# A fused attention and two-layer kernel: the first stage rebuilt, with two blocks in float32 and row scale and squares taken where the results leave PSUM

## The chip, the cores and the metric

One Trainium2 chip, of which the program uses one core. The metric is device time in microseconds (us) of one execution; less is better. The comparison can tell about 0.2% (2 us here) from no change.

## The reference, cut to what matters

```python
for t in range(S):                       # B=4, H=8, S=768, D=48
    state = alpha[:, :, t, :, None] * state + einsum('bhd,bhe->bhde', k[:, :, t], v[:, :, t])
    y[:, :, t] = einsum('bhd,bhde->bhe', q[:, :, t], state)
x = y as 3072 tokens x 384
xn = x / sqrt(mean(x * x, axis=-1) + 1e-6) * rms_g
g = xn @ w_gate                          # 384 x 1536
x = (g / (1 + exp(-g)) * (xn @ w_val)) @ w_out
h = x @ w_in                             # 384 x 2048
out = (h * cos(h)) @ w_out2
```

The weights reach the kernel as 64-bit floats, everything else as 32-bit floats.

## The kernel before, in words

The 3072 tokens are eight tiles of 384. **Attention** of a tile is four units, each a pair of heads on 112 partitions (48, a gap of 16, 48). For unit u, `att_prep` (letter p) multiplies up the decays with two scans on VectorE and scales k and q; `att_T` (T) transposes k, `att_sc0` (s) makes the scores in two PSUM banks, which ScalarE copies out and GpSimd masks; `att_u` (u) makes the state of each 128-token block, with a carry to the next tile; `att_y` (y) makes the result in PSUM and copies it into the tile `xT`, rows 0 to 47 on ScalarE, rows 64 to 111 on VectorE. The first unit of a tile (heads 6 and 7) is spread by six small DMAs (`att_fix`) over the gaps of the other three, so that `xT` has three blocks of 128 rows.

**The first layer** of a tile runs over twelve blocks f of 128 hidden columns: a gate product `pg`, a value product `pv`, Silu and product on ScalarE and VectorE, and a product into three sums `o`. Every operand is split into a high and a low word (type F32R, `xh`, `xl`, `hh`, `hl`, `g0h`, `g0l` and so on), and one product is three matmuls; a gate or value product is nine matmuls of 384 columns, an output product of one block nine too. For tiles 0 to 2 the row factor (`rms`) is multiplied in after the gate product, so that the products needn't wait for it.

**Weights** come in pieces of 768 or 384 64-bit numbers per partition (`st_g`, `st_v`, `st_o`, later `ws`). `conv_a` makes 32-bit numbers of one: ScalarE scales the low words, then the high words, VectorE joins both (`cv`). `conv_b` splits that: ScalarE copies the high word (`g0h`), VectorE subtracts for the low word (`g0l`). The second half of the first three pieces is hidden blocks 2 and 3; the pieces g1, v1, o1 follow, and those of blocks 8 to 11 (g2, v2, o2) come through three `ws` buffers, each loaded when VectorE has joined what was in it.

**Order.** The string `FIRST` is the order of tile 0's pieces, held on every engine; `i` in it is filler matmuls (`keep_clock`). After it, a counter of slots deals out conversions (`CONV`) and the attention of the next tile between the blocks of the current one. What stands in which order on an engine within these limits is decided when the program is built. SyncE issues all loads of this stage, in order.

The second layer follows from about 500 us on and isn't touched.

## Time and profile before

| | us |
|---|---|
| median of 3 runs (lowest to highest) | 995.41 (995.2 to 995.5) |
| the profiled execution, its own time | 995.65 |
| its span, first to last instruction | 993.9 |
| outside the span | 1.75 |

The rows below are of this one execution. Busy times of TensorE include a modelled tail of each matmul, so a busy TensorE may still have room; the distance between the starts of two matmuls is what one costs in a row of them.

### The profile page before, as it was taken

How to read it: one execution, taken by the hardware profiler on the slowest of the kernel's cores; microseconds unless marked ns; L12 is line 12 of the kernel's file. 1: busy time of each engine (PE TensorE's matmuls, PEld its weight loads, DVE VectorE, ACT ScalarE, POOL GpSimd, SP SyncE). 2: the span in 40 equal slices, each digit the busy share in tenths (PEclk: the TensorE clock that was granted, in tenths of full speed). 3: DMA queues.
4: the chain of work that ended last, by engine and by line, in shares of the span. 5: the costliest groups of instructions: out<-in, count | busy, mean ns of one | idle time of the engine just before them, and what ended most of it. 6: DMA issues, size and time to landing. Idle time of an engine off the chain costs nothing.

```text
span 993.9 us, 16981 instructions
## 1 busy us (share of the span) xinstructions
PE 976.8 (98%) x6451; PEld 900.6 (91%) x6451; DVE 707.3 (71%) x1333; ACT 608.8 (61%) x1270; POOL 119.1 (12%) x154
## 2 busy tenths in 40 slices
PE   8799999999999999999999999999999999999998
PEld 7698899999999999999999998888888888888886
DVE  7898786978868678678537227777767777777666
ACT  4878465565664565555633227777777677777764
POOL 3010010100110010010102211121201201211000
PEclk9999999999999999999999999999999999999999
DMA  8937234443453443544202574001010010000000
GB/s 244 328 93 203 83 92 138 125 132 93 124 152 121 135 131 102 146 137 126 89 18 88 200 305 170 18 28 38 1 43 22 1 54 12 32 1 1 33 1 32
DMA packets 44273, 96.71 MB, mean 97 GB/s; under 512 B 5520, under 2 KB 25488, under 8 KB 44192
## 3 DMA queue, kind: packets, MB, share of 16 engines
q1 hardware_dynamic: 41312, 79.90, 26.3%
q0 software_dynamic: 2880, 15.73, 4.3%
q8 instruction: 51, 0.84, 0.4%
q14 instruction: 30, 0.25, 0.1%
HBM read 69.26 MB, written 25.17 MB: 95 GB/s over the span
## 4 chain that ended last, share of the span: by engine, by line
PE 87%; DVE 6%; DMA 3%; ACT 2%; issue 1%; SPq 0%; POOL 0%; DVEq 0%; ACTq 0%; POOLq 0%
PE p L838 20%; PE pg L700 13%; PE o L700 12%; PE pv L700 12%; PE px L838 9%; PE py L838 9%; PE py L481 2%; PE pe L838 2%; DMA q<-akq 2%; PE py L486 1%; PE pu L448 1%; PE idle L534 1%; DVE cv L189 1%; PE ps L382 1%; PE ps L383 1%
## 5 line engine op out<-in xcount | busy, mean ns | idle before, releaser
L838 DVE SCALAR_TENSOR_TENSOR kk<-kk,c 128x512 f32<-128x512 int32 x192 | 148.4, 773 | 93.2 <-ACT kk L838 93.2
L838 PE MATMUL p<-hh,p 128*128 128x512 f32 x576 | 211.5, 396 | 0.2 <-ACT kk L838 0.2
L838 PEld LDWEIGHTS p<-hh,p 128*128 128x128 f32 x576 | 108.7, 189 | 17.1 <-ACT kk L838 0.3
L838 ACT ACTIVATE kk<-kk 128x512 f32<-128x512 f32 x192 | 115.7, 626 | 3.0
L838 PE MATMUL p<-hl,p 128*128 128x512 f32 x288 | 113.7, 395 | 0.2 <-DVE hl L89 0.2
L838 PE MATMUL px<-xh,i 128*128 128x256 f32 x481 | 113.8, 291 | 0.0
L838 PE MATMUL py<-xh,i 128*128 128x256 f32 x482 | 109.4, 282 | 0.0
L399 POOL TENSOR_SCALAR_AFFINE_SELECT sm<-sm 128x512 f32<-128x512 f32 (+1 forms) x64 | 47.6, 747 | 454.1 <-ACT sm L398 454.0
L838 PEld LDWEIGHTS px<-xh,i 128*128 128x128 f32 x481 | 84.2, 189 | 12.3 <-ACT py L838 12.3
L759 DVE TENSOR_TENSOR pv<-th,pv 128x384 f32<-128x384 f32 x96 | 53.3, 555 | 58.6 <-PE pv L700 51.0
L86 ACT ACTIVATE hh<-pv 128x384 fp32r<-128x384 f32 x96 | 46.9, 488 | 67.5 <-DVE pv L759 65.3
L838 PEld LDWEIGHTS py<-xh,i 128*128 128x128 f32 x482 | 84.3, 189 | 4.3 <-DVE hl L89 0.3
L746 ACT ACTIVATE th<-pg 128x384 f32<-128x384 f32 x96 | 46.8, 488 | 65.3 <-PE pg L700 45.8
L89 DVE TENSOR_TENSOR hl<-kk,hh 128x512 fp32r<-128x512 f32 x96 | 68.1, 710 | 3.3
L838 PE MATMUL px<-xl,i 128*128 128x256 f32 x240 | 67.8, 283 | 0.0
L838 PE MATMUL py<-xl,i 128*128 128x256 f32 x240 | 67.6, 282 | 0.0
L89 DVE TENSOR_TENSOR hl<-pv,hh 128x384 fp32r<-128x384 f32 x96 | 53.0, 552 | 18.3 <-ACT hh L86 17.2
L838 ACT ACTIVATE kk<-c 128x512 int32<-128x512 f32 x96 | 60.3, 628 | 1.6
L838 PEld LDWEIGHTS p<-hl,p 128*128 128x128 f32 x288 | 54.4, 189 | 5.6 <-DVE hl L89 1.0
L838 ACT ACTIVATE m<-pe 128x256 f32<-128x256 f32 x48 | 18.4, 384 | 53.8 <-PE pe L838 53.8
L838 PEld LDWEIGHTS py<-xl,i 128*128 128x128 f32 x240 | 45.2, 189 | 4.3
L838 ACT ACTIVATE c<-px 128x512 f32<-128x512 f32 x48 | 28.8, 599 | 31.7 <-PE px L838 31.6
(233 smaller groups left out, 2623.3 us busy)
## 6 DMA issues: line engine op xcount, KB each, us to landing
ak<-akq SPq DMA_DIRECT2D x29, 337.8 KB, 3.5
i<-d_i POOLq DMA_DIRECT2D x12, 768.0 KB, 6.0
ws<-w2i SPq DMA_DIRECT2D x16, 384.0 KB, 3.4
ws<-w2o SPq DMA_DIRECT2D x16, 384.0 KB, 3.4
d_p<-whl SPq DMA_DIRECT2D x32, 192.0 KB, 3.2
p<-d_p POOLq DMA_DIRECT2D x8, 768.0 KB, 6.4
v<-vin SPq DMA_DIRECT2D x32, 168.0 KB, 3.4
q<-akq SPq DMA_DIRECT2D x30, 168.0 KB, 3.0
```

Of the source, the lines that this page charges most:

```text
L86: return act.activation(out=dst, in_=src, func=AF.Copy)
L89: return eng.tensor_tensor(out=dst, in0=a, in1=h.bitcast(F32), op=ALU.subtract)
L189: done("dve", dve.scalar_tensor_tensor(out=v, in0=hi, scalar=3, in1=lo, op0=ALU.logical_shift_left, op1=ALU.bitwise_or))
L382: pe.matmul(dst, a[0], b[0], start=start, stop=False)
L383: pe.matmul(dst, a[0], b[1], start=False, stop=False)
L399: pool.affine_select(out=dst, in_=dst, pattern=[[0, n], [1, C]], compare_op=ALU.is_ge, fill=0.0, base=0, channel_multiplier=-1,)
L448: done("pe", pe.matmul(pu[r0:r1, n * D:(n + 1) * D], s["t"][:, n * R + r0:n * R + r1], s["v"][:, n, r0:r0 + D], start=True, stop=True,))
L481: pe.matmul(py[r0:r1, c], s["v"][:, n, r0:r1], s["s"][:, n, j, :], start=n == 0, stop=False)
L700: mm(dst, w[a][:, cols(kc)], rhs[kc][b], start=first and k == 0, stop=last and k == 3 * len(rhs) - 1,)
L746: done("act", act.activation(out=t, in_=p, func=AF.Silu, scale=1.0 / WS))
L759: dve.tensor_tensor(out=p, in0=t, in1=p, op=ALU.mult)
L838: last2[eng] = fn(*args, **kw).ins
```

## The change

What it does:

- Blocks 0 and 1 of tile 0 are computed in float32: the joined weights (`whole`, held in three buffers that are free at this time) and `xT` go straight into three float32 matmuls for each gate and value product, and one for each of the three output sums. Their result `hh` is written by VectorE as float32, without a split. The split of these three half pieces for the later tiles is done by `conv_whole` at slots 9, 11 and 13, and slot 0 has no conversion now.
- The row scale `rms_g` is multiplied in where tile 0's `att_y` copies PSUM out, so `x_split` of tile 0 is a plain copy and a subtraction. The first unit's scale has a layout of its own, `g3`, which six small DMAs on ScalarE's queue load; all of its rows are copied out by ScalarE.
- The squares of tile 0 are taken by ScalarE from PSUM for each of the four units, so the row sum has four parts of 112 rows and doesn't wait for `att_fix`.
- The carry of tile 0 (the last state update of each unit) is left to the end of the first stage (`carry_on`, C).
- The high words of a piece can be converted ahead of its low words (`high_first`, H). `FIRST` is a new string: among other things `i5` is `i3` and `i7` is gone, and blocks 0 and 1 are finished in it (M).
- For tiles 1 and 2 the row sum is placed ahead of the first value product instead of behind it; tile 2's first state product is placed one slot later.

The diff, cut:

```diff
-    "p0 T0 s0 i4 p1 u0 i5 p2 T1 s1 y0 S4 u1 p3 T2 s2 a0 y1 u2 T3 s3 u3 b0 a1 y2 y3 i7 x0 x1 x2 b1 g0 "
-    "q0 q1 q2 r0 r1 r2 n0 a2 a3 v0 g1 o0 P0 b2 v1 P1 b3"
+    "p0 T0 s0 i4 p1 u0 i3 T1 s1 p2 y0 S4 u1 T2 s2 p3 y1 u2 T3 s3 u3 a0 y2 H0 y3 a1 g0 r0 r1 "
+    "r2 r3 a2 n0 v0 x0 x1 x2 H0 b2 g1 o0 P0 a3 v1 M0 H0 b3 P1 M1 a4 C0"
-CONV = {0, 1, 4, 6, 8, 10, 12, 14} | set(range(16, 36))
+CONV = {1, 4, 6, 8, 10, 12, 14} | set(range(16, 36))
...
+    def conv_high(st):
+        g = st.bitcast(F32).rearrange("p (n t) -> p n t", t=2)[:, :, 1]
+        done("act", act.activation(out=g, in_=g, func=AF.Prelu, scale=HIGH_SCALE, alpha=NEG_SCALE))
+
+    def high_first():
+        st = staged[0][2]
+        conv_high(st)
+        highs.append(st)
...
+        first = key[1] == "0" and o == 0
+        v = at.tile([128, 768], I32, tag=dict(g="bdh", v="bdl", o="yn")[key[0]], name="whole") if first else cv_tile(st)
...
+    def conv_whole():
+        h, l, v = whole.pop(0)
+        split(h, l, v.bitcast(F32))
...
+            if n == 2 and i == 0:
+                carried.append((p, st[-1], s["ge"], w))
+                continue
...
-            done("act", act.activation(out=x[0:D, p, :], in_=py[0:D, :TT], func=AF.Copy))
-            done("dve", dve.tensor_copy(out=x[64:R, p, :], in_=py[64:R, :TT]))
+            if u == 0:
+                done("act", act.activation(out=x[:R, p, :], in_=py[:R, :TT], func=AF.Copy, scale=g3[:R]))
+            else:
+                done("act", act.activation(
+                    out=x[0:D, p, :], in_=py[0:D, :TT], func=AF.Copy, scale=g_sb[0:D, p:p + 1]
+                ))
+                done("dve", dve.tensor_scalar(
+                    out=x[64:R, p, :], in0=py[64:R, :TT], scalar1=g_sb[64:R, p:p + 1], scalar2=None, op0=ALU.mult
+                ))
+            t = m1.tile([128, TT], F32, tag="t" if u else "y", bufs=3 if u else 1, name="sq")
+            done("act", act.activation(out=t[:R], in_=py[:R, :TT], func=AF.Square))
...
+        if full(i, f):
+            w = wt0[a]
+            for kc in range(3):
+                o = c * 384 + kc * 128
+                done("pe", pe.matmul(p[:, :TT], w[:, o:o + 128], xT[0][:, kc, :], start=kc == 0, stop=kc == 2))
+            return p
...
+            pe.matmul(acc1[i][j][:, :TT], wt0["o"][:, k], h, start=start, stop=stop)
...
-    for u in range(4):
-        load_all(u)
+    for c in range(3):
+        for r in (0, 64):
+            act.dma_start(out=g3[r + 16 * c:r + 16 * c + 16], in_=g_in[r + 48:r + 64, c:c + 1])
+    att_load(0)
+    att_loadq(0)
+    att_load(1)
+    att_loadv(0)
+    att_loadq(1)
+    att_loadv(1)
     sp.dma_start(out=g_sb, in_=g_in)
+    load_all(2)
+    load_all(3)
...
+        if i == 0:
+            done("act", copy_r(xh[:, c, :], x))
+            done("dve", sub_r(dve, xl[:, c, :], x, xh[:, c, :]))
+            return
...
-                for x in range(2):
+                for x in order1(i)[:2]:
                     pre["g", x] = m1_mm(i, "g", x, ps_g.tile([128, 512], F32, tag="g", name="pg"))
-                    if x == 0:
-                        pre["v", 0] = m1_mm(i, "v", 0, ps_g.tile([128, 512], F32, tag="g", name="pv"))
                     late.pop(0)()
+                    if x == f:
+                        pre["v", f] = m1_mm(i, "v", f, ps_g.tile([128, 512], F32, tag="g", name="pv"))
...
+        if step[0] in (9, 11, 13):
+            with behind():
+                conv_whole()
```

Three places in the order of the instructions. The first is SyncE's queue at the program's start: `ak` and `akq` hold decays, k (and q) of a unit, in the order of units 0 to 3. Before:

```order
L332 DMA v<-vin 128x336
L314 DMA ak<-akq 112x772
L323 DMA q<-akq 112x384
L332 DMA v<-vin 128x336
L312 DMA akq<-akq 112x1156
L332 DMA v<-vin 128x336 [waits DMAHW0_49]
L312 DMA akq<-akq 112x1156 [waits DMAHW1_49]
L332 DMA v<-vin 128x336 [waits DMAHW2_49]
```

And now:

```order
L338 DMA ak<-akq 112x772
L356 DMA v<-vin 128x336 [waits DMAHW0_49]
L347 DMA q<-akq 112x384 [waits DMAHW2_49]
L356 DMA v<-vin 128x336 [waits DMAHW4_49]
L1093 DMA g_sb<-gin 128x3 [waits DMAHW5_49]
L336 DMA akq<-akq 112x1156 [waits DMAHW6_49]
L356 DMA v<-vin 128x336 [waits DMAHW7_49]
L336 DMA akq<-akq 112x1156 [waits DMAHW0_49]
```

Unit 1's `ak` stands one place earlier, unit 2's `akq` waits for a semaphore that counts unit 1's `ak` (the waits named DMAHW are for the earlier DMA that shares one of eight semaphores), and the loads behind it wait in order.

The second place is ScalarE between the last scores of tile 0 (`sm`) and the row sum's copy `nm`. Before:

```order
L398 ACTIVATE sm<-ps 128x3x128 [waits PE_49,Pool_49]
L398 ACTIVATE sm<-ps 128x3x128 [waits PE_49]
L86 ACTIVATE g0h<-cv 128x768 [waits DVE_49]
L186 ACTIVATE st_v_162<-st_v_162,low 128x768 [waits DMAHW5_49]
L188 ACTIVATE st_v_162<-st_v_162 128x768
L502 ACTIVATE xT<-py 48x384 [waits PE_49] x2
L602 ACTIVATE xh<-xT,g_sb 128x384 [waits DMAHW6_49,DMAHW7_49,DMAHW3_49,DVE_49]
L602 ACTIVATE xh<-xT,g_sb 128x384 [waits DMAHW1_49,DMAHW0_49,DVE_49]
L602 ACTIVATE xh<-xT,g_sb 128x384 [waits DMAHW3_49,DMAHW2_49,DVE_49]
L86 ACTIVATE v0h<-cv 128x768
L518 ACTIVATE sq<-xT 128x384 x3
L551 ACTIVATE nm<-rm,eps 128x96 [waits PE_49]
```

And now:

```order
L428 ACTIVATE sm<-ps 128x3x128 [waits PE_49]
L199 ACTIVATE st_g_166<-st_g_166,low 128x768 [waits DMAHW2_49]
L189 ACTIVATE st_g_166<-st_g_166 128x768
L546 ACTIVATE xT<-py,g_sb 48x384 [waits PE_49]
L553 ACTIVATE sq<-py 112x384 [waits DVE_49]
L189 ACTIVATE st_v_170<-st_v_170 128x768 [waits DMAHW3_49]
L546 ACTIVATE xT<-py,g_sb 48x384 [waits PE_49]
L553 ACTIVATE sq<-py 112x384 [waits DVE_49]
L199 ACTIVATE st_v_170<-st_v_170,low 128x768
L199 ACTIVATE st_g_274<-st_g_274,low 128x768 [waits DMAHW2_49]
L189 ACTIVATE st_g_274<-st_g_274 128x768
L603 ACTIVATE nm<-rm,eps 128x96 [waits PE_49]
```

Each unit's copy `xT` is now followed by a square that waits for VectorE's copy of the other rows, five conversions of 768 columns stand among them and ahead of `nm`, and `xh` and the split copies have moved behind it.

The third place is TensorE at the state product `pu` of tile 1's last unit, while tile 0's blocks 8 to 10 are computed. Before:

```order
L700 MATMUL pv_1220<-xl_415,v2h_813 128x384
L700 MATMUL pv_1220<-xh_414,v2l_814 128x384
L700 MATMUL o0_718<-hh_1165,o2h_902 128x384
L700 MATMUL o1_719<-hh_1165,o2h_902 128x384
L700 MATMUL o2_720<-hh_1165,o2h_902 128x384
L448 MATMUL pu_949<-v_802,th_909 64x48
L448 MATMUL pu_949<-v_802,th_909 48x48
```

And now, from behind the three matmuls `o<-hh,o2h` of the same block:

```order
L760 MATMUL pg_1205<-xh_456,g2h_681 128x384
L760 MATMUL pg_1205<-xl_457,g2h_681 128x384
L760 MATMUL o0_685<-hl_1127,o2h_863 128x384
L760 MATMUL o0_685<-hh_1126,o2l_864 128x384
L760 MATMUL o1_686<-hl_1127,o2h_863 128x384
L760 MATMUL o1_686<-hh_1126,o2l_864 128x384
L760 MATMUL o2_687<-hl_1127,o2h_863 128x384
L760 MATMUL o2_687<-hh_1126,o2l_864 128x384
L760 MATMUL pg_1205<-xh_456,g2l_682 128x384
L760 MATMUL pg_1205<-xh_456,g2h_681 128x384
L760 MATMUL pg_1205<-xl_457,g2h_681 128x384
L486 MATMUL pu_910<-v_765,th_870 64x48
```

Eleven matmuls of the first layer now stand between those three and `pu`, where none stood.

## Rows read from the trace of the kernel before

**Rows 1.** The page, parts 1 and 2: engines, and granted clock in slices.
```profile
PE 976.8 (98%) x6451; PEld 900.6 (91%) x6451; DVE 707.3 (71%) x1333; ACT 608.8 (61%) x1270; POOL 119.1 (12%) x154
PEclk9999999999999999999999999999999999999999
```

**Rows 2.** Windows: busy us of each engine, granted clock, DMA share.
```profile
19.60:30.00 10.40, 9.29 (x116) 7.16 (x117) 8.52 (x17) 9.31 (x19) 1.38 (x3) 1.00 0.93 342
40.00:50.00 10.00, 8.01 (x42) 7.12 (x43) 10.00 (x18) 10.00 (x17) 0.00 (x0) 1.00 0.90 330
50.00:60.00 10.00, 10.00 (x66) 9.20 (x65) 9.60 (x17) 6.64 (x12) 1.13 (x2) 1.00 0.28 99
80.00:90.00 10.00, 9.10 (x59) 8.60 (x59) 7.47 (x15) 8.06 (x21) 2.27 (x2) 1.00 0.77 219
90.00:100.00 10.00, 9.14 (x63) 7.74 (x64) 8.31 (x20) 7.92 (x18) 0.52 (x1) 0.83 0.77 205
```

**Rows 3.** TensorE's waits, 20 to 50 us: first and last of seven.
```profile
PE pg L700 <- ACT g0h L86: 1.1, 1, 1.1
PE pg L700 <- DVE g0l L89: 0.4, 1, 0.4
```

**Rows 4.** Timeline 0 to 20 us: start, duration, engine, line, operation.
```profile
4.08 0.43 SPq L312 DMA_DIRECT2D akq<-akq  x1
7.76 0.96 DVE L347 TENSOR_TENSOR_SCAN G<-ak,d 112x387 f32<-112x387 f32 x1 [1.30 <-DMA ak<-akq]
11.72 0.96 DVE L347 TENSOR_TENSOR_SCAN G<-akq,d 112x387 f32<-112x387 f32 x1
14.97 0.56 DVE L503 COPY xT<-py 48x384 f32<-48x384 f32 x1
16.21 0.27 DVE L458 SCALAR_TENSOR_TENSOR c<-w,ge 112x48 f32<-112x48 f32 x1
18.91 0.69 DVE L356 TENSOR_TENSOR akq<-akq 112x384 f32<-112x384 f32 x1
```

**Rows 5.** DMA issued at 4.08 us: KB, us to landing.
```profile
akq<-akq SPq DMA_DIRECT2D x1, 505.8 KB, 7.2
```

**Rows 6.** Timeline and one tile: prices of matmuls and conversions.
```profile
88.41 0.33 PE L700 MATMUL pv<-xh,v2h 128*128 128x384 f32 x1
88.59 0.33 PE L700 MATMUL pv<-xl,v2h 128*128 128x384 f32 x1
L584 PE MATMUL rm<-sq,mean x12: 483/484/591, 183.4 to 521.1; 128*128 128x384 f32 x12
41.86 1.01 ACT L186 ACTIVATE st_g<-st_g,low 128x768 int32<-128x768 uint32 x1
42.76 0.92 ACT L188 ACTIVATE st_g<-st_g 128x768 f32<-128x768 f32 x1
41.89 1.80 DVE L189 SCALAR_TENSOR_TENSOR cv<-st_o 128x768 int32<-128x768 int32 x2
```

**Rows 7.** Timeline, ScalarE: tile 0's row sum and first Silu.
```profile
29.84 0.34 ACT L551 ACTIVATE nm<-rm,eps 128x96 f32<-128x96 f32 x1 [0.49 <-PE rm L543]
35.53 0.49 ACT L746 ACTIVATE th<-pg 128x384 f32<-128x384 f32 x1 [0.87 <-DVE pg L744]
```

**Rows 8.** Timeline and a window, TensorE, 88 to 95 us.
```profile
88.76 0.34 PE L700 MATMUL pv<-xh,v2l 128*128 128x384 f32 x1
90.04 0.79 PE L700 MATMUL o<-hh,o2h 128*128 128x384 f32 x3 [0.94 <-ACT hh L86]
91.66 0.66 PE L448 MATMUL pu<-v,th 128*64 128x48 f32 x8 [0.82 <-ACT th L394]
95.00 0.44 PE L700 MATMUL pg<-xh,g2h 128*128 128x384 f32 x1
92.00:93.00 1.00, 1.00 (x16) 1.00 (x15) 1.00 (x4) 1.00 (x3) 0.00 (x0) 0.50 0.76 61
```

**Rows 9.** Timeline, TensorE: tile 1's row factors.
```profile
117.63 0.89 PE L573 MATMUL rb<-yb,ones 128*128 128x384 f32 x2 [0.59 <-DVE yb L564]
```

More of the change, by code (lines that the diff above doesn't have):

```diff
@@ L75, in fused_kernel @@
     sd = []
+    yn = []
     def make_bd():
         for i in range(1):
-            bd.append([at.tile([R, NB, 2, C], F32R, name=f"bd{x}{i}") for x in "hl"])
+            bd.append([at.tile([R, NB, 2, C], F32R, tag=f"bd{x}", name=f"bd{x}{i}") for x in "hl"])
             for t in bd[-1]:
@@ L99, in fused_kernel @@
     mean = const.tile([128, 128], F32, name="mean")
+    g3 = const.tile([128, 1], F32, name="g3")
     d1 = const.tile([R, NB, C + 1], F32, name="d1")
@@ L186, in assemble @@
         act.activation(out=lo, in_=lo.bitcast(U32), func=AF.Identity, scale=LOW_SCALE, bias=low)
-        g = hi.bitcast(F32)
-        done("act", act.activation(out=g, in_=g, func=AF.Prelu, scale=HIGH_SCALE, alpha=NEG_SCALE))
+        if st in highs:
+            highs.remove(st)
+        else:
+            conv_high(st)
         done("dve", dve.scalar_tensor_tensor(
@@ L200, in fused_kernel @@
     half = []
+    whole = []
+    wt0 = {}
     def conv_a():
@@ L206, in conv_a @@
         h, l = (x[:, o:o + st.shape[-1]] for x in wt[key][0])
-        v = cv_tile(st)
+        first = key[1] == "0" and o == 0
+        v = at.tile([128, 768], I32, tag=dict(g="bdh", v="bdl", o="yn")[key[0]], name="whole") if first else cv_tile(st)
+        if first:
+            wt0[key[0]] = v.bitcast(F32)
         assemble(st, v)
-        half.append((h, l, v))
+        (whole if first else half).append((h, l, v))
         if tag and tag != "ws":
@@ L355, in att_prep @@
         q3 = q.rearrange("p (n c) -> p n c", c=C)
[L356 to L357 removed]
+        if u >= 4:
+            dve.tensor_tensor(out=k3, in0=k3, in1=Iv.rearrange("p (n c) -> p n c", c=C + 1)[:, :, 1:], op=ALU.mult)
+        ge = at.tile([R, NB, 1], F32, tag="ge" if u >= 4 else "ge0", bufs=3 if u >= 4 else 4, name="ge")
         done("act", copy_r(ge, G[:, :, C:C + 1]))
[L359 removed]
+        ins = dve.tensor_tensor(out=q3, in0=q3, in1=G[:, :, 1:], op=ALU.mult)
+        if u < 4:
+            ins = dve.tensor_tensor(
+                out=k3, in0=k3, in1=Iv.rearrange("p (n c) -> p n c", c=C + 1)[:, :, 1:], op=ALU.mult
+            )
+        done("dve", ins)
         s.update(ge=ge, k=k, q=q)
@@ L438, in att_sc0, with carry_on @@
             causal(sm[:, :, j, :], ps[:, :TT].rearrange("p (n c) -> p n c", c=C), NB)
+    carried = []
+    def carry_on():
+        for p, x, ge, w in carried:
+            done("dve", dve.scalar_tensor_tensor(
+                out=carry[p], in0=x, scalar=ge[:, 2, :], in1=w[:, 2], op0=ALU.mult, op1=ALU.add
+            ))
     def att_u(u):
@@ L716, in fused_kernel, with order1, full, parts_w @@
     acc1 = {}
+    def order1(i):
+        return list(range(12))
     pre = {}
     post = []
+    def full(i, f):
+        return i == 0 and f < 2
+    def parts_w(key, f):
+        return wt[key][0]
     def m1_mm(i, a, f, p):
         g, c = divmod(f, 4)
+        if full(i, f):
[4 more added lines that the diff above has]
+            return p
         rhs = [(xn[i][0][:, kc, :], xn[i][1][:, kc, :]) for kc in range(3)]
         mm9(
-            p[:, :TT], wt[f"{a}{g}"][0], rhs, True, True,
+            p[:, :TT], parts_w(f"{a}{g}", f), rhs, True, True,
             lambda kc: slice(c * 384 + kc * 128, c * 384 + kc * 128 + 128),
@@ L757, in m1_val @@
         hh = m1.tile([128, TT], F32R, tag="hh", bufs=3, name="hh")
+        if full(i, f):
+            done("dve", dve.tensor_tensor(out=hh.bitcast(F32), in0=t, in1=p, op=ALU.mult))
+            hid1[i, f] = hh.bitcast(F32)
+            return
         hl = m1.tile([128, TT], F32R, tag="hl", bufs=3, name="hl")
@@ L764, in m1_unit @@
         g, c = divmod(f, 4)
-        if j == 0 and f == 0:
+        start, stop = f == order1(i)[0], f == order1(i)[-1]
+        if j == 0 and start:
             acc1[i] = [ps_o.tile([128, 512], F32, tag=f"o{n}", name=f"o{n}") for n in range(3)]
-        w = wt[f"o{g}"][0]
+        w = parts_w(f"o{g}", f)
         h = hid1[i, f]
         k = slice(c * DM + j * 128, c * DM + j * 128 + 128)
-        mm9(acc1[i][j][:, :TT], w, [h], f == 0, f == 11, lambda kc: k, mm or pe.matmul)
-        if f == 11:
+        if full(i, f):
+            pe.matmul(acc1[i][j][:, :TT], wt0["o"][:, k], h, start=start, stop=stop)
+        else:
+            mm9(acc1[i][j][:, :TT], w, [h], start, stop, lambda kc: k, mm or pe.matmul)
+        if stop:
             o = m1.tile([128, TT], F32, tag="t", bufs=3, name="x2")
@@ L785, in m1_out @@
             m1_unit(i, f, j)
-        if f == 11 and i < NRAW:
+        if f == order1(i)[-1] and i < NRAW:
             rms.pop(i)
```

48 lines of the change are left out of this document (28 added, 20 removed).

## The prediction

> **What bounds the kernel now.** I read the page first: TensorE is busy for 98% of the span [rows 1], so time can only go where it waits or does work that can be spared. The windows then show where it waits: until some 120 us. From 19.6 to 30 us it lacks 1.1 us of the window, from 40 to 50 us 2.0 us; from 50 to 60 us nothing is left, and from 80 to 100 us it lacks 1.8 us again [rows 2]. The view of TensorE's waits names the releasers between 20 and 50 us: seven, all products of the weight conversion, the splits or Silu on ScalarE and VectorE, 5.1 us in all [rows 3]. Both these engines are busy for the whole of 40 to 50 us [rows 2]: the first stage is bound by the conversion of weights, not by matmuls. Last I read TensorE's timeline around the hole at 90 us. The block's last value matmul starts at 88.76 us, the next gate product at 95.00 us, and between them stand three output matmuls, `pu` and the results `py` of one unit [rows 8]. It waits 0.94 us for `hh` and 0.82 us for `th`, both of which stand in ScalarE's queue among conversions. The window from 92 to 93 us has a granted clock of 0.50, the lower of TensorE's two levels (1.2 GHz), after 2.6 us in which it had done one us of work. The 2.98 us from the start of `py` (0.36 us after that of `pu`, at 92.02) to 95.00 would have taken half, so the clock cost some 1.5 us. The waits, the clock and what little stands between them make about 3.5 us lost of the 5.9 us from 89.1 to 95.0 us: the three matmuls cost 0.5 us and `pu` with `py` at the full clock 1.9 us (0.36 and 1.5 us).
>
> **The start.** Tile 0's attention hangs on VectorE's preparation of units 1 to 3. Unit 1's scan starts at 7.76 us, on landing of its `ak` [rows 4]. Now 168 KB less are ahead of it; by the 500 KB that take 7.2 us from issue to landing behind others [rows 5] a piece of a third of it is 0.5 to 0.8 us, so I say 7.0 us. Against it stands the queue: unit 2's `akq` was issued at 4.08 us [rows 4] and landed at 11.3 us [rows 5], just ahead of its scan at 11.72 us. It now waits for unit 1's `ak`, so it is issued at 7.0 us. If the transfers ahead still keep the engines busy, it lands at 11.3 us again; if its first bytes must wait the 2.9 us, at 14.2 us. The former is nearer, since three loads are still under way then; I take 12.1 us. From that scan to the end of unit 3's preparation (18.91 + 0.69 = 19.60 us) VectorE worked for 7.88 us without a gap. It loses the copy of unit 0's rows (0.56 us) and one carry (0.27 us) [rows 4]. So it ends at 12.1 + 7.88 - 0.83 = 19.1 us, **0.5 us earlier** (18.3 to 21.2 us by the bounds).
>
> **To the first Silu.** From here on I count from that end, E. Before, the row sum's copy `nm` starts at E + 10.24 and the first Silu at E + 15.93 us [rows 7]. Now ScalarE's queue must go through this (a low word 0.90 us to the next start, a high one about 0.8, the join on VectorE 0.90 [rows 6]; a copy or square 0.42 to 0.5 as the Silu's 0.49 [rows 7]): square of unit 1 behind VectorE's copy, `th` and masks' copies to E + 2.4; low and high of `st_g` to 4.1; `xT` of unit 2 to 4.5; then its square must wait until VectorE has joined `whole` and copied the other rows (5.5), to 6.0; high of `st_v` 6.8; `xT` of unit 3 7.2, VectorE's half 7.8, square 8.3; low of `st_v`, low and high of the second `st_g` to 10.9. Only then comes `nm`, though its sums are ready at 9. That is E + 10.9 against 10.24. Behind it VectorE first joins (0.9 us), then does the 2.95 us of row factors, then subtracts three `xl` and a `g0l` (2.5 us) before the first gate product is scaled: the first Silu is at E + 17.8, so at 36.9 us, **1.4 us later**. ScalarE and VectorE wait in this stretch for each other; I find some 4 us more idle on VectorE than before.
>
> The Trainium skill, "PSUM — Partial Sum Buffer", section "PSUM bank collisions raise a hardware error", speaks against such copies: two engines reading the same bank and quadrant of partitions at one time collide, reads included, so they are made to wait for each other. Here the square takes rows of both other readers, and the listed wait of each square on VectorE agrees; by the page alone the two half copies, in different quadrants, could overlap, which would take 0.5 us a unit off the sum.
>
> **TensorE's own work.** A split matmul of 384 columns costs 0.173 us (88.41 to 88.59) and shows 0.33 us; a float32 one is two instructions that show 0.484 us each [rows 6]. With the same tail of 0.16 us one costs 0.32 us, the pair 0.65 us. Three instead of nine: 1.95 for 1.56 us, four times, + 1.6 us; one instead of three: 0.65 for 0.52 us, six times, + 0.8 us. The row sum's fourth part is nothing to that. These 2.4 us lie in the 5.1 us of waits [rows 3] and in the place of the fillers; without that cover they cost 2.4 us. They also spare ScalarE and VectorE two splits of `hh` (1.0 us each) in the time in which these are full.
>
> **Up to 89 us.** Block 2's and 3's products need the second halves' words: value words of block 2 at 41 us, the joined output piece at 43, so that blocks 0 and 1 are summed and block 3's value product ends at 49.5 us, where before that state was reached at 51. But the conversion of the next pieces is later by VectorE's idle time, and three deferred splits (0.8 us on ScalarE, 0.9 on VectorE each) fall into 50 to 75 us, where VectorE is 96 to 100% busy [rows 2]: TensorE waits 2 us for `g1l` until 53.9 us, then runs through. By the end of block 7's products it stands at 78.7 us against 78.1 us. VectorE is then 3 us late, and TensorE only doesn't feel it as the `ws` loads were the slower ones at this place. At the end of block 9's products, 89.1 us before, I get **89.3 us**.
>
> **The hole at 90 us.** ScalarE comes to the awaited `th` at much the same time as before (I get 91.1 for 91.27 us). But ahead of `pu` stand eleven matmuls more, 11 x 0.173 = 1.9 us, which were done behind the hole. With them the wait for `th` is 0.3 us or none, TensorE doesn't fall silent for so long, and I expect no drop of the clock: of the 3.5 us lost, some 0.5 us remain, **3.3 us** won to 3.0 by the safe side. Rule and row here: the Trainium skill, "TensorE: Matmul & The Clock Gate", section "HAM oscillation — how this bites in real kernels", says that waits between bursts of matmuls throttle the array anew each time; the trace agrees in the window at 0.50. By it alone, keeping the hole's waits would keep the 1.5 us too.
>
> **Tile 1's row factors.** The broadcast `rb` waited 0.59 us for VectorE's chain at 117.63 us [rows 9], with 15 matmuls placed between row sum and broadcast. Now ten stand there: 5 x 0.173 = 0.9 us more wait, + 0.9 us, if the sum isn't taken earlier.
>
> **Sum.** + 0.2 (to 89 us), - 3.2, + 0.9 = - 2.1 us. Edits that I cost at nothing: the six small loads of `g3` on ScalarE (waits until 7 us hide their issue; without that cover about 0.4 us each as one on SyncE [rows 4]), the late carries (0.27 us each, moved from the start to 43 us, where nothing waits for them), the shift of tile 2's first state product (0 to 0.4 us). All behind 130 us is as before. From the profiled 995.65 us this gives 993.55; the median lies 0.24 us lower, so **993.3 us**.
>
> **The rivals.**
> 1. The hole stays: `th` or `hh` comes later than TensorE's new cover, because VectorE's 3 us of lateness reach ScalarE's queue. For it: both engines are full [rows 2]. Against it: the order puts 1.9 us of matmuls there. Then + 0.2 + 0.9 = + 1.1 us, 996.5 us.
> 2. Slower, by the clock of the first stage. The float32 products stand between waits, with the seven fillers of `i7` gone. If TensorE's clock falls to the lower level there or while it waits for `g1l`, its next 3 us of work, as at 92 us, take some 1.5 us more each time; with two such drops and the hole kept the sum is + 1.1 + 3.0 = + 4.1 us, 999.5 us; with one and the hole filled - 0.6. It decides the sign from the second drop on. Against it: the waits of up to 1.1 us before 50 us [rows 3] came with a full clock [rows 2].
> 3. More is won: unit 2's load lands as before and ScalarE's chain before `nm` is shorter than my sum, so E and the first Silu are 1 to 2 us earlier, the conversions follow, and the waits to 50 us shrink. Then - 2.1 - 3 = - 5.1 us, 990.3 us.
>
> **How the numbers follow.** My forecast has a chance of 0.45, its own range 991.3 to 995.3 us (E's bounds, and 0 to 1 us of the hole). Rival 1 has 0.20, rival 2 0.15, rival 3 0.20. Faster by over 0.2% is below 993.4: half of the forecast's cases and nearly all of rival 3, 0.43. Within 0.2% are the other half and most of rival 1, 0.40. Slower are rival 2 and the edge of rival 1, 0.17. The range from 989.5 to 998.0 us leaves out a part of rivals 2 and 3, under 0.2.
>
> **What would show it.** Right: unit 3's preparation ending near 19.1 us; the first Silu near 37 us; blocks 0 and 1 in float32 at 0.65 us a matmul; waits for `g1l` near 52 us; no window at 0.50 around 92 us, and the eleven matmuls ahead of `pu`; `rb` waiting about 1.5 us. Wrong: a lowered clock anywhere before 60 us, `akq` of unit 2 landing at 14 us, or TensorE still silent at 90 us.

## The result and the profile after

The changed kernel takes **1001.02 us** (median of 12 runs, 997.78 to 1004.68), the kernel before, run beside it, 995.41 us (994.94 to 997.73): a ratio of 1.0054, interval 1.0042 to 1.0066. It is slower by 5.6 us where 2.1 us less were forecast, and lies outside the range. Its runs spread more than those of before. The profiled execution is one of the quicker ones: its own time 999.22 us, its span 997.5 us, so 3.6 us above the profiled execution of before.

The page, engines and granted clock, to be held against [rows 1]:

```profile
PE 980.4 (98%) x6423; PEld 899.2 (90%) x6423; DVE 706.0 (71%) x1331; ACT 608.5 (61%) x1269; POOL 121.7 (12%) x154
PEclk9989999999999999999999999999999999999999
```

The third slice has fallen. The windows show where (as [rows 2]: busy us of each engine, granted clock, DMA share):

```profile
20.00:30.00 10.00, 7.28 (x92) 4.49 (x90) 4.50 (x7) 8.08 (x14) 0.99 (x2) 0.92 0.99 355
30.00:40.00 10.00, 9.09 (x30) 5.51 (x29) 8.15 (x19) 6.05 (x10) 0.00 (x0) 0.91 1.05 331
50.00:60.00 10.00, 8.26 (x38) 7.32 (x38) 10.00 (x17) 7.84 (x13) 2.44 (x2) 0.66 0.30 121
90.00:100.00 10.00, 10.00 (x80) 9.27 (x79) 8.64 (x18) 9.12 (x22) 1.15 (x2) 1.00 0.72 201
```

From 90 to 100 us TensorE is full and at full clock: the hole of [rows 8] is closed. But from 50 to 60 us, where it lacked nothing, it now lacks 1.7 us, and its clock of 0.66 means some 6.8 us at the lower level. VectorE is busy for all of these 10 us.

TensorE's timeline (start, duration, in brackets the idle time before) shows that stretch. One split matmul is 0.17 us apart at the full clock and 0.32 at half:

```profile
43.61 4.09 PE L851 MATMUL o<-hh,whole 128*128 128x384 f32 x12
47.24 0.63 PE L760 MATMUL pv<-xh,v0h 128*128 128x384 f32 x1
...
50.55 0.38 PE L422 MATMUL pt<-ident,ak 112*128 112x112 f32 x2 [1.26 <-issue]
...
53.05 0.66 PE L486 MATMUL pu<-v,th 128*64 128x48 f32 x8 [1.19 <-ACT th L424]
53.64 1.65 PE L465 MATMUL ps<-q,ak 48*128 48x128 f32 x6
55.22 0.69 PE L760 MATMUL pg<-xh,g1l 128*128 128x384 f32 x1
...
58.58 0.52 PE L760 MATMUL o<-hh,o0l 128*128 128x384 f32 x1
58.90 0.43 PE L760 MATMUL o<-hl,o0h 128*128 128x384 f32 x1
```

What TensorE waits for at 53.05 us is `th` of tile 1's attention. For the wait of 1.26 us the profile names no releaser, but it ends 0.10 us after VectorE has finished the `ak` of that attention (49.92 + 0.53 us, below), which `pt` transposes. So both waits are for tile 1's attention. That attention starts late. In the kernel before, its first scan, its third unit's load and the `ws` load behind that:

```profile
41.01 0.96 DVE L347 TENSOR_TENSOR_SCAN G<-ak,d 112x387 f32<-112x387 f32 x1
```
```profile
67.54 0.33 SPq L314 DMA_DIRECT2D ak<-akq  x1
71.12 0.35 SPq L168 DMA_DIRECT2D ws<-wg  x1
```

And now the same loads on SyncE, and VectorE:

```profile
75.79 0.33 SPq L338 DMA_DIRECT2D ak<-akq  x1
76.22 0.38 SPq L170 DMA_DIRECT2D ws<-wg  x1
```
```profile
43.42 0.80 DVE L474 SCALAR_TENSOR_TENSOR c<-w,ge 112x48 f32<-112x48 f32 x4
44.14 0.95 DVE L371 TENSOR_TENSOR_SCAN G<-ak,d 112x387 f32<-112x387 f32 x1
...
49.92 0.53 DVE L381 TENSOR_TENSOR ak<-ak 112x384 f32<-112x384 f32 x1
...
53.09 0.95 DVE L90 TENSOR_TENSOR g1l<-cv,g1h 128x768 fp32r<-128x768 f32 x1
...
76.03 0.94 DVE L90 TENSOR_TENSOR o1l<-cv,o1h 128x768 fp32r<-128x768 f32 x1
79.06 0.96 DVE L371 TENSOR_TENSOR_SCAN G<-ak,d 112x387 f32<-112x387 f32 x1 [2.08 <-DMA ak<-akq]
```

The first scan is at 44.14 us (before 41.01), directly behind the four late carries (`c`); the third unit's load is issued at 75.79 us (before 67.54) and VectorE stands 2.08 us for it. The `ws` load queued behind it goes out at 76.22 us (before 71.12). The load waits until a unit's scores have read the buffer. Before, those scores are one row of twelve matmuls from 66.53 us; now six start at 71.14 and six at 74.83 us, with fifteen of the first layer's matmuls between them:

```profile
66.53 0.94 PE L435 MATMUL ps<-q,ak 48*128 48x128 f32 x12
```
```profile
71.14 0.93 PE L465 MATMUL ps<-q,ak 48*128 48x128 f32 x6
...
74.83 0.93 PE L465 MATMUL ps<-q,ak 48*128 48x128 f32 x6
```

So of its 8.2 us, about 4.6 are the scores' lateness and 3.7 their second half's place in the order.

### The profile page after: what moved, and what is told of

Read it like the earlier page. It is cut to its first block, busy times and chain, and to the rows that moved or that the text cites. A ratio compares the mean times of both kernels' runs of the same rounds, so it can differ in the third digit from the quotient of the medians.

```text
span 997.5 us, 16935 instructions
## 1 busy us (share of the span) xinstructions
PE 980.4 (98%) x6423; PEld 899.2 (90%) x6423; DVE 706.0 (71%) x1331; ACT 608.5 (61%) x1269; POOL 121.7 (12%) x154
## 4 chain that ended last, share of the span: by engine, by line
PE 84%; DVE 6%; DMA 5%; ACT 4%; issue 1%; SPq 0%; DVEq 0%; ACTq 0%
PE p L921 20%; PE pg L760 12%; PE pv L760 12%; PE o L760 12%; PE px L921 9%; PE py L921 9%; PE pe L921 2%; PE py L522 2%; PE py L527 2%; DMA st_g<-wg 1%; PE pu L486 1%; DMA q<-akq 1%; DVE G L371 1%; DMA d_i<-whl 1%; PE ps L412 1%
## 5 line engine op out<-in xcount | busy, mean ns | idle before, releaser
L429 POOL TENSOR_SCALAR_AFFINE_SELECT sm<-sm 128x512 f32<-128x512 f32 (+1 forms) x64 | 50.0, 785 | 420.1 <-ACT sm L428 416.5
L921 ACT ACTIVATE m<-pe 128x256 f32<-128x256 f32 x48 | 18.4, 384 | 53.9 <-PE pe L921 53.9
```

The source lines that it names most:

```text
L429: pool.affine_select(out=dst, in_=dst, pattern=[[0, n], [1, C]], compare_op=ALU.is_ge, fill=0.0, base=0, channel_multiplier=-1,)
L921: last2[eng] = fn(*args, **kw).ins
```

## The experiments

Each was timed in five rounds beside the kernel before; ratio with its 95% interval. The runs named "before" are edits of the kernel before, the others of the changed one.

| run | median us | before | ratio |
|---|---|---|---|
| after_again | 1001.73 | 994.55 | 1.0070 [1.0053, 1.0087] |
| fill_first_gap | 1005.23 | 994.55 | 1.0109 [1.0092, 1.0125] |
| fill_both_gaps | 1001.27 | 994.55 | 1.0066 [1.0049, 1.0083] |
| before_no_fillers | 997.00 | 994.55 | 1.0021 [1.0007, 1.0036] |
| hold_earlier_7 | 1000.13 | 995.43 | 1.0048 [1.0035, 1.0060] |
| hold_earlier_10 | 999.37 | 995.43 | 1.0045 [1.0032, 1.0057] |
| old_row_sum_place | 1002.52 | 995.43 | 1.0077 [1.0063, 1.0090] |
| split_on_gpsimd | 1006.17 | 995.43 | 1.0117 [1.0101, 1.0133] |
| no_float32 | 1003.77 | 996.07 | 1.0083 [1.0065, 1.0101] |
| fix_on_scalar_queue | 1000.17 | 996.07 | 1.0042 [1.0026, 1.0058] |
| before_hold_later | 1002.39 | 996.07 | 1.0061 [1.0046, 1.0077] |
| hold_10_and_fillers | 999.59 | 996.07 | 1.0035 [1.0023, 1.0047] |
| squares_later | 996.75 | 995.78 | 1.0009 [0.9997, 1.0021] |
| squares_later_hold_10 | 1002.56 | 995.78 | 1.0069 [1.0054, 1.0085] |
| before_hold_e5 | 994.86 | 995.78 | 0.9986 [0.9977, 0.9996] |
| before_hold_e2 | 996.55 | 995.78 | 1.0013 [1.0004, 1.0021] |
| squares_twice | 1001.91 | 995.82 | 1.006 [1.004, 1.008] |
| squares_later_filled | 996.26 | 995.82 | 1.0008 [0.9997, 1.0019] |

**The clock of the first stage.** Four runs put fillers into TensorE's waits, or take them out. The changed kernel again, without an edit:

> The changed kernel once more, to see how far its own executions differ. Theory A (the clock): the profiled execution lost 1.7 us to a clock of 0.50 from 28.7 to 31.5 us and some 3.1 us to another from 52.4 to 59.2 us; each of the two stretches of waits before them is at the edge, so other executions should show other numbers or lengths of half-clock stretches, and their times should spread as before, 998 to 1004 us, with a longer time where more half clock is seen. Theory B (the clock is not it, late conversions are): the same two places wait in each execution, and the times spread without any relation to the clock.

Fillers in the wait at 20 to 30 us; then four matmuls of zeros ahead of block 3's value product too; and the kernel before without its fillers:

```diff
-    "... u3 a0 y2 H0 y3 a1 g0 r0 r1 r2 r3 a2 n0 v0 x0 ..."
+    "... u3 a0 y2 H0 y3 a1 i7 g0 r0 r1 r2 r3 a2 n0 i3 v0 x0 ..."
```

> Ten filler matmuls put back where TensorE waits from 23.0 to 29.0 us (seven ahead of the first gate product, three behind the row sum), no other instruction moved. Theory A: the clock stays at 1.00 from 20 to 40 us, the first gate product starts up to 1.4 us later but its third part, which waits for xT until 26.5 us, does not; 1.4 to 1.7 us less, so 997.5 us against 999.2, and less spread; the second drop near 52 us remains. Theory B: no change, or up to 1 us more.

```diff
+    def fill_zero(n):
+        for _ in range(n):
+            pe.matmul(acc1[0][0][:, :128], ones, zero..., start=False, stop=False)
...
+            if (i, f) == (0, 3):
+                fill_zero(4)
```

> As fill_first_gap, and four more matmuls (with zeros, added into the first output sum) ahead of block 3's value product, so that the wait of 1.26 us at 49.3 us is filled with work; VectorE changes the place of two operations of block 3 and unit 4 by one. Theory A: if this is enough to hold the clock over the next wait (1.19 us at 51.9 us), another 3.1 us less than fill_first_gap, some 994.4 us, below the kernel before by about 1 us; if only part of it, the drop comes later or is shorter. Theory B: the same as fill_first_gap or up to 1 us more.

```diff
-    "... a1 y2 y3 i7 x0 x1 x2 b1 g0 "
+    "... a1 y2 y3 x0 x1 x2 b1 g0 "
```

> The kernel before without its seven fillers at 24.5 us, nothing else moved in the first 300 us. Theory A: if it is the missing fillers that let the clock fall in the changed kernel, it falls here too, near 27 to 31 us, + 1.4 to 1.7 us, 997 us; if the clock holds, the float32 products with their waits for xT in between are needed for the drop as well. Theory B: 0, or 0.2 us less, as the first gate product no longer stands behind fillers.

The repeated kernel gives the best measure of the clock by chance. Up to block 3 its profiled execution runs beside the first one. Silu of blocks 0, 3, 4 of tile 0 and of tile 1 in the first execution, and then in the repeated one, ScalarE's timeline:

```profile
36.40 0.49 ACT L821 ACTIVATE th<-pg 128x384 f32<-128x384 f32 x1 [0.75 <-DVE pg L819]
47.97 0.47 ACT L821 ACTIVATE th<-pg 128x384 f32<-128x384 f32 x1
61.32 0.48 ACT L821 ACTIVATE th<-pg 128x384 f32<-128x384 f32 x1
122.52 0.95 ACT L821 ACTIVATE th<-pg 128x384 f32<-128x384 f32 x2 [0.29 <-DVE pg L819]
```
```profile
36.45 0.49 ACT L821 ACTIVATE th<-pg 128x384 f32<-128x384 f32 x1 [1.48 <-DVE pg L819]
48.04 0.47 ACT L821 ACTIVATE th<-pg 128x384 f32<-128x384 f32 x1
60.23 0.48 ACT L821 ACTIVATE th<-pg 128x384 f32<-128x384 f32 x1
120.98 0.95 ACT L821 ACTIVATE th<-pg 128x384 f32<-128x384 f32 x2 [0.29 <-DVE pg L819]
```

and its windows:

```profile
20.00:30.00 10.00, 7.30 (x93) 4.54 (x94) 4.45 (x7) 8.09 (x14) 0.99 (x2) 1.00 0.97 367
30.00:40.00 10.00, 8.13 (x28) 4.74 (x27) 8.16 (x19) 6.13 (x10) 0.00 (x0) 1.00 1.00 319
50.00:60.00 10.00, 8.17 (x44) 7.26 (x45) 10.00 (x18) 8.10 (x14) 2.44 (x2) 0.83 0.31 122
```

In the repeat the clock is full from 20 to 40 us, and the Silu at 36.45 us is no earlier: the first drop cost nothing. From 50 to 60 us it has 0.83 in place of 0.66, which is 1.7 us of clock; by block 4 it is 1.1 us ahead, at tile 1 1.5 us. The second drop cost nearly its face value. Two other traces with the same order at this place agree: from block 3's to block 4's Silu it takes 12.2 us in the repeat and in `fill_first_gap`, both with 1.7 us of missing clock there, and 13.4 and 13.7 us in the first execution and in `squares_twice`, both with 3.4 us.

One kernel has thus different drops in different executions. Over the first 12 runs the product of span and missing clock is 4.0 us on average; in the 91 runs of the kernel before that were timed beside the variants it is 1.8 us. The expectation's question, whether time goes with the clock, can be answered from the 18 executions of the changed kernel: 0.74 us more for each us of missing clock (correlation 0.66), and 998.3 us at none. The kernel before stands near 995 us. So the lowered clock goes with a part of the loss, and some 3 us are there without it. A correlation alone doesn't say which of the two is the cause.

The fillers did what they were to do (no drop from 20 to 40 us, TensorE idle 0.45 us from 20 to 30 instead of 2.7) and won nothing: the first of these two kernels, in which nothing but the fillers differs, is some 4 us slower than the changed one, the second as slow as it. A drop stands at 55 us and a new one at 123.6 us, and ahead of that ScalarE waits 3.1 and 2.4 us for the six small transfers of tile 1 (1.17 us in the changed kernel). Without its fillers the kernel before is slower by 0.2%, at the edge of what can be told; its profiled execution (993.85 us, one of its quicker ones) has an early drop and none at 92 us.

**Where tile 1's attention is released.** Its pieces up to a certain slot wait for the last operations of ScalarE and VectorE in the first stage (`held[0]`). Here this mark is taken seven, then ten pieces of the string earlier:

```diff
-    for pc in att_pieces(0):
+    first = att_pieces(0)
+    for k, pc in enumerate(first):
...
-    held[0] = ahead[0] = (mark["act"], mark["dve"])
+        if k == len(first) - 7:
+            held[0] = (mark["act"], mark["dve"])
+    ahead[0] = (mark["act"], mark["dve"])
```

> In the changed kernel the attention of tile 1 is held behind the last ScalarE and VectorE operations of the first stage; its first scan starts at 44.2 us against 41.0 us before, and the load of its third unit's ak, which waits for scores of its first unit, is issued at 74.7 us against 67.5 us, so that VectorE stands 2.35 us for it and the conversions of blocks 8 to 11 end 5 us later. Here the hold is set seven pieces earlier (behind the second conversion of a value product's weights and block 0's Silu). Theory C (the late start of tile 1's attention costs the time, by way of the late ak and the waits from 100 to 125 us): the first scan starts near 41 us, ak is issued by 71 us, no wait of VectorE for it, waits of TensorE from 100 to 130 us fall from 2.2 to 4.1 us to about 1.5 us, and the median falls by 2 to 4 us, to 997 to 999 us. Theory A (the clock alone): no change beyond 1 us but what the half-clock stretches give.

> As hold_earlier_7, with the hold ten pieces from the end, so that tile 1's attention comes even earlier among the first stage's work. Theory C: ak issued still earlier; the first stage is delayed by VectorE's work for tile 1 (1 to 2 us at the first products), what follows is no later than before, 996 to 999 us. Theory A: as the changed kernel, 1001 us.

The first scan came to 39.38 and 36.71 us and the third load to 71.10 and 69.23 us, without the wait of 2.08 us in the first. The ratios, 1.0048 and 1.0045, are 0.0006 to 0.0025 below the two of the changed kernel (1.0054 and 1.0070): about 1 us, where 2 to 4 were expected. What was won there was lost elsewhere. In the first, ScalarE waited 3.21 us for the small transfers, `rb` 2.19 us, and the clock was at half from 119.5 us on; in the second, tile 0's Silus came up to 7.5 us later (block 5's at 72.06 us against 64.56). So undoing the late start does not undo the loss. Two runs put the other suspects to the test, the place of the row sum and the fillers together with the earlier mark:

```diff
-                for x in order1(i)[:2]:
+                for x in range(2):
+                    if x == 0:
+                        pre["v", 0] = m1_mm(i, "v", 0, ...)
```

> The row sum of tile 1 back behind the first value product, so that 15 instead of 10 matmuls stand between it and its broadcast; nothing else in the order differs. By the prediction's term the wait for the row factors falls from 1.5 to 0.6 us, - 0.9 us, 1000.4 us if the rest is unchanged. If the wait is hidden by other work or the sum is then later by the same time: 0.

> hold_earlier_10 with the ten fillers of fill_first_gap between 23 and 29 us. Theory A: no half clock between 20 and 45 us, 0 to 1.7 us less than hold_earlier_10, 998 to 999.4 us. If filled gaps are given back by later waits as in fill_first_gap: 999.4 us or more.

The old row sum's place moved the sum by one matmul row only and left `rb` waiting 1.7 us, so it tells nothing of the 0.9 us. Fillers and the earlier mark together are no better than the mark alone.

The strongest run of this kind takes the suspected cost to the kernel before. There the mark is taken later, behind slot 0's join; no other line of the kernel changes:

```diff
-                conv_piece()
+                conv_a()
+                if step[0] == 0:
+                    held[0] = (mark["act"], mark["dve"])
+                conv_b()
```

> The kernel before with one suspected cost added alone: tile 1's attention is held behind the conversion that follows the first stage, so that its first scan starts some 3 us later (near 44 us instead of 41), as in the changed kernel. Theory C: ak of tile 1's third unit is issued at 72 us or later instead of 67.5, the weights of blocks 8 to 11 are late, and the median rises by 2 to 4 us, to 997 to 999 us. Theory A and theory D: no change beyond 1 us.

It costs 6 us, the whole loss of the change. Its scans and ScalarE's wait for the small transfers:

```profile
43.14 0.96 DVE L347 TENSOR_TENSOR_SCAN G<-ak,d 112x387 f32<-112x387 f32 x1
...
79.80 0.96 DVE L347 TENSOR_TENSOR_SCAN G<-ak,d 112x387 f32<-112x387 f32 x1 [2.01 <-DMA ak<-akq]
```
```profile
107.04 0.52 ACT L518 ACTIVATE sq<-xT 128x384 f32<-128x384 f32 x1 [4.32 <-DMA xT<-xT]
```
```profile
50.00:60.00 10.00, 9.15 (x50) 8.22 (x48) 9.85 (x17) 5.56 (x10) 0.52 (x1) 0.83 0.26 104
```

A first scan at 43.14 us brings the late third load, VectorE's wait of 2 us for it and a lowered clock between 50 and 60 us, all three as in the changed kernel. But with the mark the build changes the order on TensorE, ScalarE and VectorE up to some 180 us, and this has costs of its own: ScalarE waits 4.32 us for the transfers (1.5 before), and six matmuls instead of 15 stand between tile 1's row sum and `rb`, which waits 2.16 us instead of 0.59. The run shows that a later mark, with the order that comes of it, is enough for a loss of this size. It doesn't price the delay alone.

The mark taken earlier in the kernel before:

> The kernel before with tile 1's attention held five pieces earlier in the first stage. If the kernel before is itself bound by that start, the third unit's ak is issued before 67 us and the median falls by 1 to 3 us, 993 to 995 us. If the first stage's conversions are delayed by as much: within 1 us of before. If any other order costs time (the order of before being the best of several): slower by 1 to 4 us.

> As before_hold_e5 with the hold two pieces from the end: the first scan of tile 1 some 1 to 2 us earlier than 41.0 us. If the start decides: 0 to 2 us faster; if any other order costs time: slower by 1 to 4 us.

Five pieces earlier is 0.14% faster than the kernel before, the only ratio below 1, though its first scan comes 4.7 us earlier (36.35 us) and its third load 5.1 us (62.43 us); two pieces earlier is 0.13% slower. Both are below the 0.2% that can be told.

**Single parts.** The deferred low word on GpSimd, the stage without float32, and tile 1's six transfers on ScalarE's queue:

```diff
-        split(h, l, v.bitcast(F32))
+        done("act", copy_r(h, v.bitcast(F32)))
+        sub_r(pool, l, v.bitcast(F32), h)
```

> The three deferred subtractions for the low words of blocks 0 and 1 on GpSimd instead of VectorE, 0.95 us each taken from VectorE between 54 and 71 us. Theory C in the form that VectorE's load delays tile 1's attention: third ak issued 1 to 2 us earlier, half to all of the wait of 2.35 us gone, median 1 to 3 us lower. If only the start of tile 1's attention matters: within 1 us of the changed kernel.

```diff
-        first = key[1] == "0" and o == 0
+        first = False
...
-        return i == 0 and f < 2
+        return False
```

> The changed kernel with blocks 0 and 1 of tile 0 in split words again: their weights are split at once (with places b0 and b1 in the string, ahead of the first products), no float32 products, no deferred splits; row scale and squares at PSUM, the loads, the late carries stay. Theory D (float32 with its late splits is what costs the time): back to 995 to 996 us. Theory C (the late start of tile 1's attention, which the end of the first stage holds, and what follows from it): as the changed kernel within 2 us, 999 to 1002 us, if tile 1's first scan still starts at 44 us or later.

```diff
-            sp.dma_start(out=x[48:64, c, :], in_=x[16 * c:16 * c + 16, 3, :])
+            eng = act if i == 1 else sp
+            eng.dma_start(out=x[48:64, c, :], in_=x[16 * c:16 * c + 16, 3, :])
```

> The six small transfers that fill the gaps of tile 1's xT are issued on ScalarE's own queue instead of SyncE's, where they stand behind the loads of weights and of tile 2. In the slower profiled executions of the changed kernel's order ScalarE stood 2.4 and 3.1 us for them near 103 us with scores' copies behind it, in the faster ones 1.1 us. If this transfer decides between the fast and the slow executions: a wait of about 1 us or less, the median 1 to 2 us lower (999 to 1000 us) and less spread. If not: 1001 us, or more by what ScalarE's issues cost (about 0.5 us each).

The first two are slower than the changed kernel. Without float32 the first Silu is at 38.31 and tile 1's first scan at 49.26 us (in its slowest execution, the profiled one). So split words bring nothing back here; as they delay the attention further, the run doesn't price float32 alone. The third cut ScalarE's wait for the transfers to 0.45 us; its ratio is 0.0012 below the changed kernel's first, with intervals that overlap.

**ScalarE's waits at the squares.** The prediction had ScalarE wait for VectorE's copy at each square, as the listed waits and the section of the Trainium skill's "PSUM — Partial Sum Buffer" on "PSUM bank collisions raise a hardware error" (accesses of two engines to one bank and quadrant collide, so they need a semaphore between them) had it. It does; ScalarE's waits between 15 and 35 us in the changed kernel:

```profile
ACT sq L553 <- DVE xT L549: 2.8, 3, 1.2
```

The overlap of the two half copies, which the prediction held possible, didn't come: VectorE's copy for unit 3 starts at 25.79 us, 0.03 us behind the end of ScalarE's, for which VectorE waited 1.80 us.

In the next run the squares of units 1 to 3 are pieces of their own (q), placed where VectorE's copy is done; the second adds the mark ten pieces earlier:

```diff
-    "... T3 s3 u3 a0 y2 H0 y3 a1 g0 r0 r1 "
+    "... T3 s3 q1 u3 a0 y2 H0 q2 y3 a1 q3 g0 r0 r1 "
...
+            def square0(u=u, py=py):
+                t = m1.tile([128, TT], F32, tag="t" if u else "y", bufs=3 if u else 1, name="sq")
+                done("act", act.activation(out=t[:R], in_=py[:R, :TT], func=AF.Square))
+                rms.setdefault(0, []).append(t)
```

> The changed kernel with the squares of units 1 to 3 placed behind the next conversion or copies on ScalarE, so that ScalarE doesn't stand for VectorE's copy of the other rows (0.90, 1.23 and 0.69 us in the profile of the changed kernel). Theory E (the mutual waits of the first stage make everything after it late): first Silu about 1.5 us earlier (near 35 us), tile 1's first scan at 43 us or earlier, the median 1 to 3 us lower, 998 to 1000 us. If the waits only move to another operation: first Silu within 0.5 us of 36.4 us, 1001 us.

> squares_later with tile 1's attention held ten pieces earlier. If the late start of tile 1's attention and the waits at the squares are the whole loss: 995 to 997 us, no slower than the kernel before. If something else costs time: 998.5 to 1000 us, as hold_earlier_10.

`squares_later` brings the changed kernel to the time of before, 996.75 us, better than expected, though its first scan is still at 43.15 us and its clock from 50 to 60 us is 0.66 again. With the earlier mark this is lost: block 1's Silu comes at 42.96 us, 2.8 us later. Two last runs ask what won the 4.3 us. One keeps the squares at the later places but takes each twice, with which the build gives TensorE, VectorE, GpSimd and SyncE exactly the order that they have in the changed kernel; the other adds four matmuls of zeros ahead of block 3's value product, which leaves the order as it is:

```diff
                 done("act", act.activation(out=t[:R], in_=py[:R, :TT], func=AF.Square))
+                if u in (1, 2, 3):
+                    done("act", act.activation(out=t[:R, :384], in_=py[:R, :384], func=AF.Square))
```

> The squares of units 1 to 3 stand later as in squares_later, but each is taken twice (the second result is written over by the same values; ScalarE has three more squares of some 0.4 us). With that the order written out at the build is that of the changed kernel on every engine but ScalarE. If squares_later gained because ScalarE no longer stands at the squares (2.8 us there in the changed kernel), then 1.2 us of it are taken up by the doubles and the rest stays: first Silu by 35.9, time 997.5 to 999. If it gained because the build chose another order further down, nothing of the gain remains: 1000.5 to 1002, with the third load of tile 1's attention again issued after 75 us and VectorE waiting some 2 us for it.

> squares_later with four matmuls of zeros ahead of block 3's value product, where TensorE waits 1.3 us at 49.6 just before its half clock of 52.3 to 59.1; the order is otherwise unchanged. If that wait decides the drop, TensorE is at full clock from 50 to 60, which saves up to 3.4 us of its time, and if nothing takes it back the time is 993 to 995, below the kernel before. If time gained there is given back later, as in the two kernels with filled gaps, or the drop only moves, 996 to 998.

`squares_twice` is as slow as the changed kernel. ScalarE's wait at the squares is gone, VectorE's wait for the third load is not:

```profile
ACT sq L555 <- DVE xT L550: 0.4, 1, 0.4
```
```profile
75.91 0.95 DVE L90 TENSOR_TENSOR o1l<-cv,o1h 128x768 fp32r<-128x768 f32 x1
79.07 0.96 DVE L371 TENSOR_TENSOR_SCAN G<-ak,d 112x387 f32<-112x387 f32 x1 [2.21 <-DMA ak<-akq]
```

And VectorE at the same place in `squares_later`:

```profile
74.72 0.96 DVE L90 TENSOR_TENSOR o1l<-cv,o1h 128x768 fp32r<-128x768 f32 x1
75.59 0.55 DVE L90 TENSOR_TENSOR g2l<-cv,g2h 128x384 fp32r<-128x384 f32 x1
77.49 0.57 DVE L823 TENSOR_TENSOR pg<-pg,y 128x384 f32<-128x384 f32 x1 [1.35 <-PE pg L764]
77.97 0.55 DVE L204 SCALAR_TENSOR_TENSOR cv<-ws 128x384 int32<-128x384 int32 x1
78.43 0.55 DVE L90 TENSOR_TENSOR hl<-pv,hh 128x384 fp32r<-128x384 f32 x1
78.90 0.95 DVE L371 TENSOR_TENSOR_SCAN G<-ak,d 112x387 f32<-112x387 f32 x1
```

The load is as late there (issued at 75.19 us, 75.69 in `squares_twice`), but four operations stand ahead of the scan that follows `o1l` at once in the changed kernel. From 60 to 130 us TensorE then has 0.6 us of idle time instead of 2.8 in `squares_twice`; the two profiled spans differ by 2.7 us (994.9 and 997.6). The larger part of these 2.2 us is not at the load but at tile 1's row factors. In `squares_twice`, as in the changed kernel, ten matmuls stand between row sum and `rb`:

```profile
PE rb L631 <- DVE yb L622: 1.5, 1, 1.5
```

In `squares_later` nineteen do, and `rb` doesn't wait at all. The rest, 0.7 us, is a wait for `g2h`. So the waits at the squares, which I had taken for the root, are not what the 4.3 us are: their removal made the build choose another order behind 50 us, and that order covers the late load on VectorE and the wait at `rb`. The doubles themselves explain 0.5 us at most, the lateness up to that load. In `squares_later_filled` the clock from 50 to 60 us rises to 0.83; tile 1's first Silu is 1.1 us earlier, the last sine 0.5 us, the median 0.5 us, which can't be told from nothing.

## Why the prediction was wrong

**Right.** The start: unit 1's scan came at 7.42 us and unit 2's load was issued at 7.31 us (forecast 7.0 for both, so 0.3 us were won where the estimate said 0.5 to 0.8), unit 2's scan came at 11.39 (12.1), unit 3's preparation ended at 18.26 us (19.1). ScalarE's chain to `nm` took 11.16 us from there (10.9), the first Silu is at 36.40 us (36.9). Float32 matmuls cost 0.65 us in `pg` (three in 1.94 us) and 0.61 us in `o` (six in 3.63 us) against 0.65. The hole: the last value product of block 9 ends 4.9 us later than before (93.67 + 0.17 = 93.84 against 88.93), the eleven matmuls stand ahead of `pu`, and behind them the lateness is 98.41 - 1.9 - 95.00 = 1.5 us; so 3.4 us were won there, 3.0 to 3.3 forecast, without a drop of the clock. `rb` waits 1.49 us (1.5 forecast). The timeline that answers to [rows 8] and [rows 9]:

```profile
93.67 0.34 PE L760 MATMUL pv<-xh,v2l 128*128 128x384 f32 x1
...
98.41 0.44 PE L760 MATMUL pg<-xh,g2l 128*128 128x384 f32 x1
...
120.47 0.88 PE L625 MATMUL rb<-yb,ones 128*128 128x384 f32 x2 [1.49 <-DVE yb L616]
```

**The step that failed** is "Up to 89 us", costed at + 0.2 us; it measures + 4.9. With - 3.4 at the hole and + 0.9 at `rb`, where - 3.2 and + 0.9 were put, the three terms make + 2.4 of the 2.85 us by which tile 1's first Silu is late. Two things in the step were wrong. First, "TensorE waits 2 us for `g1l` until 53.9 us, then runs through": `g1l` was ready at 54.0 us (53.09 + 0.95), but TensorE had stood 1.26 and 1.19 us for tile 1's `ak` and `th`, ran at half clock from 52.3 to 59.1 us, and its first `g1l` matmul came at 55.22 us. That is rival 2's mechanism, at the place that it named; I gave it 0.15 because waits of 1.1 us before 50 us had come with a full clock. By the two executions of one kernel 1.7 us of missing clock there cost 1.5 us; at that price the 3.4 us of the profiled execution are some 3 us of the 4.9, an estimate. Rival 2's other half, a drop in the float32 products, occurred (0.92 and 0.91) and cost nothing. That the total lands near its 999.5 us is a coincidence: it had kept the hole.

Second, "the late carries ... moved ... to 43 us, where nothing waits for them" and "TensorE only doesn't feel it". The end of the first stage is what releases tile 1's attention, so something does wait for it. The carries themselves stand directly ahead of its first scan and hold it 0.7 us. That scan is 3.1 us late, the third load 8.2 us; attention products that had kept TensorE full from 50 to 60 us [rows 2] now come with waits, and VectorE stands 2.1 us for the load. `before_hold_later` shows that such a delay, with the order that the build makes of it, is enough for a loss of this size, a lowered clock included. The reverse wasn't found: `hold_earlier_7` and `hold_earlier_10` bring scan and load forward and win back about 1 us, and `squares_later` is as quick as before with the late scan, the late load and the clock of 0.66 all in it; its block 9 ends at 93.23 us, 4.3 us late, and by tile 1's first Silu (120.39 us) it is only 0.7 us late: from 60 to 130 us TensorE has 0.6 us of idle time at full clock, where the kernel before has 3.0 us and the drop at 92 us. So it is shown that these waits stood in the stretch that was costed at + 0.2 us. How much of the 5.6 us is the late start's own stays open. I had followed TensorE, ScalarE and VectorE there by the conversions, and never asked what starts the next tile.

**Behind 130 us** "all as before" was nearly right: the lateness is 2.85 us at tile 1's first Silu (119.67 to 122.52), 2.57 at tile 7's, 3.53 at the last sine. For the 0.7 us that come in the second layer (2.83 at its first sine) I found no wait that answers to them; they stay open.

The medians differ by 5.6 us, the profiled executions by 3.6; from the traces I can only account for the latter. The rest lies in executions without a trace. Also open is how much of a variant's time is its order: most edits of the first stage move rows far behind it, and variants with nearly the same work spread from 995 to 1006 us. That the float32 blocks, without this, are worth the 3.4 us at 90 us wasn't shown either: no version of the changed kernel beat the kernel before.

## What to carry to other kernels

When a stage is rebuilt, look up what its last operation releases (a mark, a buffer, the next tile's loads) and cost that lateness through the next stage, at every wait that it feeds, before calling anything behind the stage unchanged. A gain at one hole is worth what is left after the work that used to cover the others has moved. Where a build chooses the order, an edit that removes a wait should be followed by one that removes the same wait with the order held fixed: only then is the wait's own price known.

## What the hardware showed unexpectedly

The same kernel on the same inputs had its clock lowered in different places: 28 to 32 and 52 to 59 us in one profiled execution, only within 50 to 60 us (0.83) in the other, with tile 0's first four Silus and tile 1's first scan within 0.1 us of each other. And a lowered clock isn't always worth its face value: 1.7 us of missing clock cost nothing at 28 us, where TensorE waits for conversions anyway, and 1.5 us at 55 us.
